# Attention probabilities transposed in 64x128 tiles, and the sinks' products in the two halves of the array

## The chip, the cores and the metric

The kernel runs on one core of one Trainium2 chip. The time is the device time of the program in microseconds (us); the median of three runs is compared. The engines are named as in the profile: PE is TensorE (matmuls; PEld its weight loads), DVE is VectorE, ACT is ScalarE, POOL is GpSimd, SP is SyncE, which issues most of the transfers.

## What is computed

Attention over 4 batches, 8 heads, 768 positions and heads of 64, in which a query sees the last 128 positions and the first 4 (the sinks), and behind it a gated convolution of the 512 wide result with two projections. Cut to what matters:

```python
scores = scale * np.matmul(q, k.transpose(0, 1, 3, 2))
keep = is_sink | in_window              # pos < 4, or 0 <= rel < 128
a = np.exp(np.where(keep, scores, -1e9) - max)
a = a / (np.sum(a, axis=-1, keepdims=True) + 1e-09)
attn = np.matmul(a, v)
...
gate = 1.0 / (1.0 + np.exp(-causal_conv5(x, conv_w)))
return gate * (x @ w_val) @ w_out       # x: attn, heads side by side
```

## The kernel before

The work is cut into 24 steps: 4 batches, 3 blocks of 256 query positions (`p`), 2 groups of four heads (`qd`). In a step the four heads are two pairs `g` of two heads `j`; the 256 positions are two chunks `c` of 128. Two steps (both `qd`) make one unit `m` of the gated part, of which there are 12.

One step goes through these stages; the short names are those of the order table, the lines those of the profile:

- `s0`, `s1` (L391): scores of a pair of heads on TensorE, in tiles of 64 rows by 32 columns, eight of which fit in the array, into one of two PSUM pairs of banks (`pr`). VectorE merges the window's two triangles (L396) and takes the maxima (L400, or L405 in the first `qd`).
- `e0`, `e1` (L416): exponentials on ScalarE with their sums; `rec` (L422, L423): the reciprocal.
- `norm` (L431 to L438): GpSimd multiplies by it. The window's probabilities go to a tile `wx` as two halves `n` of 64 key columns each; those of the sinks go to `skb`, in three parts (the value, its rounded part, the difference).
- `tx` (L449): TensorE transposes `wx`. For each `n`, `g` and `c` one transpose of 128 query positions by 128 (two heads of 64 key columns), with the 128x128 identity: eight in a step. The data are the weights that are loaded, the identity is what streams. The results fill both banks of a `pr` pair, half `n` in bank `n`.
- `px` (L477, L479): VectorE copies bank 0 twice into the tile `wt`, masked for the current and for the earlier block; `py` (L486): ScalarE copies bank 1. So the two engines read one bank each.
- `sk` (L454), `ts` (L462 or L464): the sinks' probabilities are transposed (128x128) and copied out into `skt`, masked by chunk.
- `vl` (L504): the product with the values in tiles of 64x64, four in the array: rows by head `j`, columns by the place in the output; PSUM bank by pair `g`. Each of them runs over one, two or three blocks of 64 queries.
- `si` (L511): the sinks' product is added: for each pair `g` one matmul of 128x128 weights (`vh`, L257 and L259, from the transfer `vsk`) over 256 positions. `vh` holds the sinks' values of both pairs, with zeros for the pair that is not meant.
- `xc`, `xh`, `hd`, `xl` (L518, L526, L530, L534): the result is copied out and split into a high and a low part; `c4`, `c0`, `c1` (L539, L547) and `th` are the convolution and the gate.
- `v0` to `v3` (L566): the value projection of a unit, 12 matmuls of 128x128 weights over 256 positions each; `g`, `h`, `l` (L585, L591, L595) gate it and split it; `o0` to `o3` (L606): the output projection, six matmuls over 512 columns each; `t0`, `t1` (L610, L613): the result is copied and stored.

Around these stand the decoding of the two weight matrices (`wva.0` to `wof.3`, L137 to L183) in the first part, some matmuls of zeros (`fill`, L224), and the loads `kq`, `vv`.

All engines follow one table, `ORDER`: a list of some thousand event names, written out, in which each event emits its instructions in the order of the list, with no scheduler behind it. So each engine's queue is fixed by that list, and semaphores set the rest. Scores and transposes share the two `pr` pairs in turn; `sk`, the projections and the weights' decoding share two other banks.

A mark such as `128*128` behind a matmul in the profile is the shape of the tile of the array that it uses, rows by columns. Below, a "change of shape" is a matmul whose tile has another shape than that of the matmul ahead.

Of the kernel before, what the change touches and what calls it, by code (L numbers as in the profile page):

```python
# [37 lines left out]
wvc.0 s1.0 wve.0 fill.4 wva.1 wvb.1 e0.0 wva.2 e1.0 wvb.2 wvc.2 fill.7 wvd.1 wol.0 kq.2 s1.1 wvc.1 rec.0 wvl.3
s0.1 fill.10 s1.2 wvf.0 woa.0 e1.1 wve.1 e0.1 wob.0 norm.0 tx.0 px.0 e1.2 woc.0 rec.1 py.0 vv.0 fill.6 sv.0
sk.0 ts.0 wod.0 wva.3 norm.1 s0.2 e0.2 vl.0 kq.8 kq.3 s0.3 wvf.1 si.0 xc.0 woe.0 wvb.3 xh.0 tx.1 c4.0 rec.2  # L40
wof.0 wol.2 wol.1 wvc.3 fill.6 hd.0 wvd.2 wve.2 px.1 wvd.3 kq.4 wve.3 e0.3 c0.0 c1.0 woa.1 wob.1 wvf.2 norm.2
vv.3 py.1 vv.1 sv.1 xl.0 tx.2 py.2 sk.1 px.2 woc.1 ts.1 vl.1 s1.3 wvf.3 wod.1 si.1 xc.1 c4.1 sk.2 ts.2 s0.4
hd.1 xh.1 xl.1 c0.1 woe.1 e1.3 wol.3 rec.3 woa.3 c1.1 wob.3 e0.4 v0.0 v1.0 th.0 y0.0 norm.3 vv.2 g0.0 vl.2
woa.2 wob.2 h0.0 l0.0 th.1 s1.4 kq.6 kq.5 wof.1 woe.3 e1.4 v2.0 v3.0 y1.0 tx.3 py.3 si.2 xc.2 woe.2 hd.2 xh.2
g1.0 px.3 wof.2 wod.2 s0.6 c4.2 c0.2 h1.0 o0.0 l1.0 o2.0 e0.6 wof.3 s0.5 c1.2 rec.4 xl.2 s1.6 wod.3 o1.0 o3.0
t0.0 norm.4 sk.3 e0.5 ts.3 t1.0 vl.3 si.3 xh.3 xc.3 xl.3 s1.5 e1.6 tx.4 px.4 vv.5 sk.4 ts.4 hd.3 c4.3 c0.3
e1.5 rec.5 norm.5 v0.1 v1.1 y0.1 py.4 c1.3 th.2 v2.1 v3.1 g0.1 h0.1 kq.7 s0.7 vv.4 th.3 vl.4 y1.1 g1.1 vv.6
l0.1 s1.7 rec.6 sv.6 s1.8 h1.1 si.4 xh.4 l1.1 xc.4 hd.4 e0.7 o2.1 o3.1 c4.4 c0.4 xl.4 e1.8 kq.10 kq.9 c1.4
norm.6 tx.5 o0.1 t1.1 py.5 o1.1 px.5 sk.5 e1.7 tx.6 rec.7 px.6 ts.5 t0.1 py.6 vl.5 si.5 xc.5 hd.5 xh.5 s0.9
e0.9 sk.6 ts.6 s0.8 e0.8 c4.5 c0.5 c1.5 xl.5 vv.7 v0.2 rec.8 v1.2 norm.7 tx.7 py.7 px.7 th.4 g0.2 v2.2 s1.9  # L50
s1.10 norm.8 th.5 h0.2 e1.9 vl.6 si.6 sk.7 vv.8 v3.2 ts.7 xc.6 hd.6 xh.6 l0.2 g1.2 rec.9 o0.2 c4.6 h1.2 l1.2
# [795 lines left out]
```

## Time and profile before

| | |
|---|---|
| median of 3 runs | 271.12 us (270.26 to 271.2) |
| the profiled execution: its time | 270.55 us |
| its span, first to last instruction | 268.7 us |
| TensorE busy | 258.3 us, 96%, 3760 matmuls |
| VectorE, ScalarE, GpSimd busy | 205.4, 189.1, 176.2 us |
| granted TensorE clock, mean | 0.991 |
| last matmul ends at | about 262 us |

The profile is one execution on the chip. Its groups name a line, an engine, an operation, `out<-in` and the shape, then how often it ran, the busy time and the mean length of one, then the idle time of the engine just ahead of it and who ended that. The length of a matmul in it contains the way through the array, so the lengths of neighbours overlap; a pace is read from start to start. A transposing matmul (L449, L454) is one record; one of full 32-bit numbers that isn't transposing (L391, L504) is two.

### The profile page before, as it was taken

The numbers are of one execution on the slowest core, as the hardware profiler recorded it, in microseconds if no ns is written. First come the engines' busy times: TensorE is split into PE (matmuls) and PEld (weight loads), VectorE is DVE, ScalarE is ACT, GpSimd is POOL, SyncE is SP. The second block draws the span as 40 slices with busy tenths as digits, with TensorE's granted clock in tenths as the row PEclk, the third lists the DMA queues.
The fourth block names the chain that finished last, engine by engine and source line by source line (L and its number), as shares of the span: only waits on it lengthen the run. The fifth ranks groups of instructions, "written<-read, shape, count | busy, mean of one in ns | idle before, by whom it ended". The sixth has DMA issues, their size and how long they took to land.

```text
span 268.7 us, 9474 instructions
## 1 busy us (share of the span) xinstructions
PE 258.3 (96%) x3760; PEld 213.6 (79%) x3760; DVE 205.4 (76%) x561; ACT 189.1 (70%) x667; POOL 176.2 (66%) x233
## 2 busy tenths in 40 slices
PE   7899999999999999999999999999999999999990
PEld 3356578789879888879879889889879889898970
DVE  6977989979869878998778788889478857834530
ACT  3899998897888867857676778968567757442420
POOL 6187986876948785675669464895776774816330
PEclk9999999999999999999999999999999999999996
DMA  7998633039344043318833619053335211040202
GB/s 220 370 384 267 239 105 104 0 112 348 107 133 168 1 158 120 131 40 290 262 115 98 196 66 305 3 146 115 111 132 201 59 44 40 1 139 2 78 14 75
DMA packets 27394, 36.93 MB, mean 137 GB/s; under 512 B 2256, under 2 KB 23760, under 8 KB 27344
## 3 DMA queue, kind: packets, MB, share of 16 engines
q1 hardware_dynamic: 26528, 35.48, 39.9%
q10 hardware_dynamic: 816, 0.79, 0.9%
q8 instruction: 31, 0.51, 0.8%
q14 instruction: 19, 0.16, 0.2%
HBM read 29.97 MB, written 6.29 MB: 135 GB/s over the span
## 4 chain that ended last, share of the span: by engine, by line
PE 83%; ACT 9%; POOL 2%; DMA 2%; issue 1%; DVE 0%; POOLq 0%; ACTq 0%
PE ac L606 25%; PE ac L566 25%; PE xv L504 11%; PE pr L391 10%; PE pr L449 7%; ACT w L416 4%; PE xv L511 3%; DMA raw<-in_w_val_dram 2%; PE ac L454 1%; POOL xl L534 1%; ACT wvh L151 1%; ACT wv_p L137 1%; ACT wv_p L156 1%; ACT wvl L183 1%; POOL wo_f L157 0%
## 5 line engine op out<-in xcount | busy, mean ns | idle before, releaser
L547 DVE SCALAR_TENSOR_TENSOR sg<-xv,cw,sg 128x256 f32<-128x256 f32 x192 | 77.8, 474 | 12.4 <-POOL sg L539 7.0
L431 POOL TENSOR_TENSOR wx<-w,sm 128x512 f32<-128x512 f32 x48 | 49.1, 1044 | 11.3 <-DVE sm L423 11.1
L416 ACT ACTIVATE w<-pr,ngm 128x132 f32<-128x132 f32 x136 | 48.5, 369 | 1.7
L595 POOL TENSOR_TENSOR gl<-sg,gh 128x512 fp32r<-128x512 f32 x24 | 31.0, 1295 | 28.1 <-ACT gh L591 28.0
L566 PE MATMUL ac<-xh,wvh 128*128 128x256 f32 x192 | 48.4, 286 | 0.0
L566 PE MATMUL ac<-xh,wvl 128*128 128x256 f32 x192 | 47.1, 279 | 0.0
L606 PE MATMUL ac<-woh,gh 128*128 128x512 f32 x96 | 39.2, 408 | 0.0
L539 POOL TENSOR_TENSOR sg<-xt,cw 128x512 f32<-128x512 f32 x24 | 25.0, 1043 | 20.6 <-ACT xt L518 20.6
L606 PE MATMUL ac<-wol,gh 128*128 128x512 f32 x96 | 38.0, 396 | 0.0
L606 PE MATMUL ac<-woh,gl 128*128 128x512 f32 x96 | 38.0, 395 | 0.0
L566 PEld LDWEIGHTS ac<-xh,wvh 128*128 128x128 f32 x192 | 36.1, 188 | 0.8 <-issue 0.5
L566 PEld LDWEIGHTS ac<-xh,wvl 128*128 128x128 f32 x192 | 36.2, 188 | 0.2
L391 PE MATMUL pr<-k,q 64*32 64x168 f32 x1536 | 35.3, 307 | 0.7 <-DMA q<-in_qt_dram 0.6
L504 PEld LDWEIGHTS xv<-wt,v 64*64 64x64 f32 x1024 | 30.4, 133 | 7.0 <-issue 4.5
L504 PE MATMUL xv<-wt,v 64*64 64x192 f32 (+2 forms) x1024 | 34.5, 278 | 0.2 <-PE ac L566 0.2
L534 POOL TENSOR_TENSOR xl<-xt,xh 128x512 fp32r<-128x512 f32 x24 | 30.8, 1289 | 3.2 <-ACT xh L526 2.8
L566 PE MATMUL ac<-xl,wvh 128*128 128x256 f32 x192 | 30.7, 280 | 0.4 <-POOL xl L534 0.4
L391 PEld LDWEIGHTS pr<-k,q 64*32 64x32 f32 x1536 | 23.8, 106 | 7.9 <-issue 2.6
L396 DVE COPY_PREDICATED pr<-low,pr 128x256 f32<-128x256 uint8 x48 | 20.3, 423 | 12.2 <-PE pr L391 12.2
L591 ACT ACTIVATE gh<-sg 128x512 fp32r<-128x512 f32 x24 | 15.0, 628 | 19.2 <-DVE sg L585 19.2
L416 ACT ACTIVATION_READ_ACCUMULATOR w<-pr,ngm 128x1 f32 x136 | 27.6, 203 | 0.0
L518 ACT ACTIVATE xt<-xv 128x512 f32<-128x512 f32 x24 | 14.4, 600 | 17.3 <-PE xv L511 17.2
(135 smaller groups left out, 495.6 us busy)
## 6 DMA issues: line engine op xcount, KB each, us to landing
k<-in_kt_dram SPq DMA_DIRECT2D x23, 408.0 KB, 5.2
v<-in_vt_dram SPq DMA_DIRECT2D x16, 384.0 KB, 4.5
out_dram<-osb SPq DMA_DIRECT2D x24, 256.0 KB, 2.2
q<-in_qt_dram SPq DMA_DIRECT2D x23, 256.0 KB, 5.4
raw<-in_w_out_dram SPq DMA_DIRECT2D x4, 512.0 KB, 6.7
v<-in_vt_dram SPq DMA_DIRECT2D x8, 256.0 KB, 5.2
raw<-in_w_val_dram SPq DMA_DIRECT2D x3, 512.0 KB, 7.3
vs<-in_vsk_dram SPq DMA_DIRECT2D x8, 128.0 KB, 5.1
```

The costliest lines, as they stand in the source:

```text
L391: nc.tensor.matmul(ss[e * QB:(e + 1) * QB, j, c * n + x0:c * n + x1], q[js, g, (4 * c + e) * QB:(4 * c + e + 1) * QB], k[js, g, (2 * c + e ...
L396: nc.vector.copy_predicated(sv[:, :, :, :D], low[:, None, None, :].to_broadcast([P, 2, 2, D]), sv[:, :, :, 2 * HB:])
L416: nc.scalar.activation(out=w[:, g, j, c], in_=sx[:, j, c, :PK], func=AF.Exp, scale=0.125 if whole else -1.0, bias=ngm[:, g, j, c:c + 1], a ...
L431: nc.gpsimd.tensor_tensor(out=t[:, n].rearrange("p c h x -> p h c x"), in0=w[:, :, :, at], in1=sm.to_broadcast([P, 4, 2, D]), op=ALU.mult)
L449: nc.tensor.transpose(out=x[:, n, o:o + P], identity=ident, in_=ws[s][:, n, c, 2 * g:2 * g + 2].rearrange("p j x -> p (j x)"))
L504: nc.tensor.matmul(acc[o * D:(o + 1) * D, g, x0 + h * D:x0 + (h + a1 - a0 + 1) * D], v[js, g, n], t[js, g, n, a0:a1 + 1].rearrange("p a r ...
L534: nc.gpsimd.tensor_tensor(out=half(xls, s, "xl", F32R), in0=xts[s], in1=half(xhs, s, "xh", F32R).bitcast(F32), op=ALU.subtract)
L539: nc.gpsimd.tensor_tensor(out=half(sg, s, "sg", F32), in0=xts[s], op=ALU.mult, in1=cw[:, g, KT - 1:].to_broadcast([P, 2, PQ]))
L547: nc.vector.scalar_tensor_tensor(out=g, in0=x, scalar=a, in1=g, op0=ALU.mult, op1=ALU.add)
L566: nc.tensor.matmul(acc[:, h], a[:, kc, cs], x[:, kc], start=(n == 0), stop=(n == 11))
L595: nc.gpsimd.tensor_tensor(out=gl, in0=g, in1=gh.bitcast(F32), op=ALU.subtract)
L606: nc.tensor.matmul(acc, a[:, kc, ts], x[:, kc], start=(kc + n == 0), stop=(kc + n == 5))
```

## The change

Three things change.

The transposes: `tx` makes 16 transposes a step instead of eight, each of 64 query positions (one half `r` of the partitions) by 128, with a 64x64 block of the identity. Rows 0 to 63 use the upper half of the array, 64 to 127 the lower, with all 128 columns: a tile of 64x128. The half `r` goes to PSUM bank `r`. So `px` and `py` read both banks, and the layout of `wt` follows: `px` stays two operations of the same sizes, `py` becomes two copies, one for each half.

The sinks: `skb` is ordered by pair `g` first, so that after the transpose pair 0 lies in partitions 0 to 63 and pair 1 in 64 to 127. The product `si` of a pair then needs 64 rows, and the two pairs' matmuls use the two halves of the array, each into its own bank. `vsk` and `vh` become half as large (no zeros for the other pair), and the correction of `vh`'s third part becomes two operations on GpSimd.

The order: the table `ORDER` is written anew. The lines behind it move by one, from the transposes on by 3 to 7: L391 is now L392, L449 is L452, L454 is L460, L504 is L510, L511 is L518, L566 is L573, L606 is L613, L486 is L491.

```diff
-NR = 8 * NSK
+NR = 4 * NSK
...
-blanks wvl.0 load_conv kq.0 masks signs leads fill.5 wvl.1 conv_weights wvl.2 wva.0 wvb.0 s0.0 kq.1 wvd.0
+fill.5 blanks load_conv masks signs leads wvl.0 kq.0 conv_weights wva.0 wvb.0 wvc.0 wvl.1 wvd.0 s0.0 s1.0
...
-            vraw[b, qd] = x = p2.tile([P, 2, P], F32, name="vs", tag="vs", bufs=2)
+            vraw[b, qd] = x = p2.tile([P, P], F32, name="vs", tag="vs", bufs=2)
...
-        vs[b, qd] = h = p2.tile([P, 2, P], F32R, name="vh", tag="vh", bufs=3)
+        vs[b, qd] = h = p2.tile([P, P], F32R, name="vh", tag="vh", bufs=3)
         nc.scalar.activation(out=h, in_=x, func=AF.Copy)
-        r = slice(2 * NR, 3 * NR)
-        nc.gpsimd.tensor_tensor(out=h[r], in0=x[r], in1=h[r].bitcast(F32), op=ALU.subtract)
+        for g in range(2):
+            r = slice(g * D + 2 * NR, g * D + 3 * NR)
+            nc.gpsimd.tensor_tensor(out=h[r], in0=x[r], in1=h[r].bitcast(F32), op=ALU.subtract)
...
-        sk = [skb[s % 2][:, n * NR:(n + 1) * NR] for n in range(3)]
-        nc.gpsimd.tensor_tensor(out=sk[0].rearrange("p (h c n) -> p h c n", c=2, n=NSK), in0=w[:, :, :, D:HB],
-                                in1=sm.to_broadcast([P, 4, 2, NSK]), op=ALU.mult)
+        sk = [skb[s % 2].rearrange("p (g k r) -> p k g r", g=2, r=NR)[:, n] for n in range(3)]
+        w, sm = (x.rearrange("p g j c x -> p g (j c) x") for x in (wn[s][0], wn[s][2][:, :, :, :, None]))
+        nc.gpsimd.tensor_tensor(out=sk[0].rearrange("p g (h n) -> p g h n", n=NSK), in0=w[:, :, :, D:HB],
+                                in1=sm.to_broadcast([P, 2, 4, NSK]), op=ALU.mult)
...
-                    o = (2 * g + c) * P
-                    nc.tensor.transpose(out=x[:, n, o:o + P], identity=ident,
-                                        in_=ws[s][:, n, c, 2 * g:2 * g + 2].rearrange("p j x -> p (j x)"))
+                    for r in range(2):
+                        rs, o = slice(r * D, (r + 1) * D), (4 * n + 2 * c + g) * D
+                        nc.tensor.transpose(out=x[:, r, o:o + D], identity=ident[rs, rs],
+                                            in_=ws[s][rs, n, c, 2 * g:2 * g + 2].rearrange("p j x -> p (j x)"))
+
+    def turned(s, n):
+        return trs[s].rearrange("p r (n x d) -> p n r x d", n=2, x=4)[:, n]
...
     def probs_x(s):
-        h0 = 2 if steps[s][1] == 0 else 0
-        t = prob(s)
-        x = trs[s][:, 0].rearrange("p (g h r) -> p g h r", g=2, r=D)
-        nc.vector.tensor_tensor(out=t[:, :, 2:6, 0], in0=x, in1=cur[:, None, None, :].to_broadcast([P, 2, 4, D]),
-                                op=ALU.mult)
-        nc.vector.tensor_tensor(out=t[:, :, h0:4, 2], in0=x[:, :, h0:],
-                                in1=prev[:, None, None, :].to_broadcast([P, 2, 4 - h0, D]), op=ALU.mult)
+        c0 = 1 if steps[s][1] == 0 else 0
+        t, x = prob(s), turned(s, 0)
+        for k, c, a, m in ((1, 0, 0, cur), (c0, c0, 2, prev)):
+            nc.vector.tensor_tensor(out=t[:, :, k:k + 2 - c, :, a].rearrange("p r k g d -> p r (k g) d"),
+                                    in0=x[:, :, 2 * c:], op=ALU.mult,
+                                    in1=m[:, None, None, :].to_broadcast([P, 2, 4 - 2 * c, D]))
...
     def probs_y(s):
-        h0 = 1 if steps[s][1] == 0 else 0
-        t = prob(s)
-        x = trs[s][:, 1].rearrange("p (g h r) -> p g h r", g=2, r=D)
-        nc.scalar.activation(out=t[:, :, 1 + h0:5, 1], in_=x[:, :, h0:], func=AF.Copy)
+        t, x = prob(s), turned(s, 1)
+        for r in range(2):
+            c = 1 if steps[s][1] + r == 0 else 0
+            nc.scalar.activation(out=t[:, 1 - r, r + c:r + 2, :, 1].rearrange("p k g d -> p (k g) d"),
+                                 in_=x[:, r, 2 * c:], func=AF.Copy)
...
         for g in range(2):
-            nc.tensor.matmul(accs[s][:, g, KT - 1:], vs[b, qd][:, g],
-                             skt[s].rearrange("p c r -> p (c r)"), start=False, stop=True, skip_group_check=True)
+            gs = slice(g * D, (g + 1) * D)
+            nc.tensor.matmul(accs[s][:, g, KT - 1:], vs[b, qd][gs], skt[s][gs].rearrange("p c r -> p (c r)"),
+                             start=False, stop=True, skip_group_check=True)
```

What the new table does to the engines' queues is seen in the built programs' orders (each row an instruction, `xN` for N alike; no time is in it). TensorE before, around the transposes of step 3: the end of a value projection, the transposes, the sinks' products of step 2, the scores of a later step, an output projection.

```order
L566 MATMUL ac_93<-xl,wvh 128x256 x4
L449 MATMUL pr_87<-ident,wx 128x128 x8
L511 MATMUL xv<-skt,vh 128x256 x2
L391 MATMUL pr_86<-k,q 32x168 x16
L606 MATMUL ac_92<-woh,gh 128x512
L606 MATMUL ac_92<-wol,gh 128x512
```

The same place afterwards:

```order
L573 MATMUL ac_93<-xl,wvh 128x256 x4
L518 MATMUL xv<-skt,vh 128x256 x2
L452 MATMUL pr_87<-ident,wx 128x64 x16
L392 MATMUL pr_86<-k,q 32x168 x16
L613 MATMUL ac_92<-woh,gh 128x512
L613 MATMUL ac_92<-wol,gh 128x512
```

The sinks and the transposes have changed places and now have one shape, so the shape changes ahead of the pair and behind it; before, it changed only around the scores. TensorE near the end of the program before (values and sinks of step 21, transposes of step 23):

```order
L504 MATMUL xv<-wt,v 64x128 x4
L504 MATMUL xv<-wt,v 64x64 x4
L511 MATMUL xv<-skt,vh 128x256 x2
L449 MATMUL pr_87<-ident,wx 128x128 x8
L606 MATMUL ac_93<-woh,gh 128x512
L606 MATMUL ac_93<-wol,gh 128x512
```

And afterwards:

```order
L510 MATMUL xv<-wt,v 64x64 x4
L452 MATMUL pr_86<-ident,wx 128x64 x16
L452 MATMUL pr_87<-ident,wx 128x64 x16
L518 MATMUL xv<-skt,vh 128x256 x2
L613 MATMUL ac_93<-woh,gh 128x512
L613 MATMUL ac_93<-wol,gh 128x512
```

The transposes of two steps now stand together with the sinks' products, with one change of shape ahead of all three and one behind. ScalarE around the copy `py` of an early step before (`vc`, `sg`, `gh` belong to the gated part):

```order
L422 ACTIVATE sm<-sm 128x8
L572 ACTIVATE vc<-ac_93 128x512
L486 ACTIVATE wt<-pr_86 128x2x4x64
L552 ACTIVATE sg<-sg 128x512
L591 ACTIVATE gh<-sg 128x512
```

And afterwards:

```order
L579 ACTIVATE vc<-ac_92 128x512
L598 ACTIVATE gh<-sg 128x512
L491 ACTIVATE wt<-pr_86 128x4x64 x2
L417 ACTIVATE w,sm<-sx,ngm 128x132 x4
L559 ACTIVATE sg<-sg 128x512
```

One copy of 512 elements a partition has become two of 256, and four exponentials now stand directly behind it.

More of the change, by code (lines that the diff above doesn't have):

```diff
@@ L36 @@
 ORDER = """
-blanks wvl.0 load_conv kq.0 masks signs leads fill.5 wvl.1 conv_weights wvl.2 wva.0 wvb.0 s0.0 kq.1 wvd.0
[L38 to L51, printed above, removed]
@@ L77 @@
-ts.23 v2.10 v3.10 g0.10 c4.22 hd.22 c0.22 c1.22 th.21 g1.10 h0.10 l0.10 o2.10 vv.23 vl.23 h1.10 si.23 xc.23
-hd.23 xh.23 l1.10 xl.22 o0.10 o1.10 c4.23 c0.23 xl.23 t0.10 c1.23 o3.10 v0.11 th.22 v1.11 t1.10 v2.11 v3.11
-g0.11 th.23 g1.11 h0.11 l0.11 o2.11 h1.11 l1.11 o0.11 o1.11 flag t0.11 o3.11 t1.11
+fill.5 blanks load_conv masks signs leads wvl.0 kq.0 conv_weights wva.0 wvb.0 wvc.0 wvl.1 wvd.0 s0.0 s1.0
+fill.10 wve.0 wva.1 wvl.2 wvb.1 e0.0 wva.2 wvd.1 e1.0 wvc.1 wvb.2 wvf.0 wvc.2 kq.1 s0.1 rec.0 norm.0 fill.7
@@ new lines @@
+e0.1 wol.0 woa.0 kq.2 s1.1 e1.1 s1.2 e1.2 fill.4 wve.1 tx.0 fill.6 wob.0 woc.0 px.0 vv.0 sv.0 sk.0 kq.4 s0.2
+py.0 rec.1 norm.1 ts.0 kq.3 vl.0 wvl.3 wva.3 s0.3 si.0 wod.0 woe.0 e0.2 xh.0 wvf.1 tx.1 xc.0 wof.0 c4.0 hd.0
+fill.6 wvb.3 rec.2 wvc.3 px.1 wvd.2 wve.2 kq.6 wvd.3 e0.3 wve.3 vv.1 wol.1 norm.2 wvf.2 woa.1 c0.0 py.1 tx.2
+c1.0 vv.3 sv.1 py.2 sk.1 wob.1 ts.1 woc.1 px.2 vv.2 wod.1 vl.1 s1.3 wvf.3 si.1 xc.1 c4.1 sk.2 ts.2 s0.4 hd.1
+xh.1 c0.1 xl.0 e1.3 rec.3 c1.1 wol.3 woa.3 kq.7 wob.3 th.0 woe.1 wof.1 xl.1 v0.0 v1.0 y0.0 norm.3 g0.0 wol.2
@@ new lines @@
+vl.8 si.8 e0.12 vv.12 vv.10 xc.8 hd.8 c4.8 xh.8 s1.11 e0.11 e1.11 kq.15 xl.8 sk.9 ts.9 c0.8 c1.8 th.7 v2.3
+v3.3 g1.3 h1.3 o2.3 s1.12 s1.13 e1.12 norm.10 l1.3 rec.12 vl.9 si.9 xc.9 c4.9 tx.10 hd.9 px.10 o3.3 xh.9
+rec.11 xl.9 norm.11 py.10 c0.9 c1.9 o0.3 t1.3 o1.3 t0.3 sk.10 ts.10 s0.13 tx.11 py.11 e0.13 px.11 vl.10 si.10
+v0.4 v1.4 xc.10 hd.10 xh.10 c4.10 sv.12 th.9 kq.18 c0.10 vv.11 norm.12 th.8 g0.4 vv.13 c1.10 kq.14 v2.4 h0.4
+v3.4 g1.4 sk.11 l0.4 ts.11 tx.12 vl.11 py.12 px.12 s0.14 h1.4 s1.14 si.11 scalars sk.12 ts.12 th.10 e1.13
@@ new lines @@
+rec.13 l1.4 o0.4 o1.4 xc.11 hd.11 c4.11 sv.13 xh.11 vv.14 e0.14 o2.4 e1.14 c0.11 o3.4 t1.4 c1.11 s0.18 s0.15
+vl.12 t0.4 th.11 si.12 xc.12 hd.12 norm.13 tx.13 xl.10 px.13 xh.12 xl.11 v2.5 rec.14 c4.12 v3.5 v0.5 py.13
+v1.5 c0.12 e0.18 c1.12 g1.5 g0.5 e0.15 norm.14 warm_up sk.13 ts.13 xl.12 h0.5 s1.15 e1.15 s1.18 l0.5 vl.13
+si.13 o0.5 kq.16 rec.15 kq.19 s0.16 tx.14 vv.17 px.14 h1.5 xc.13 hd.13 xh.13 th.12 l1.5 e0.16 c4.13 o2.5 o3.5
+o1.5 py.14 vv.15 c0.13 c1.13 t1.5 sk.14 ts.14 xl.13 e1.18 s1.16 rec.18 kq.20 vl.14 t0.5 si.14 xc.14 hd.14
@@ new lines @@
+norm.15 xh.14 tx.15 px.15 e1.16 py.15 c4.14 sk.15 ts.15 kq.17 c0.14 c1.14 rec.16 norm.16 v0.6 vv.16 v1.6 v2.6
+g0.6 s0.17 s0.19 th.13 h0.6 e0.17 xl.14 vl.15 si.15 l0.6 v3.6 g1.6 s1.19 xc.15 hd.15 kq.21 h1.6 l1.6 s1.17
+xh.15 sk.16 ts.16 o0.6 tx.16 xl.15 c4.15 e1.19 o1.6 px.16 c0.15 c1.15 kq.22 e1.17 norm.18 rec.17 vv.19 th.14
+v0.7 v1.7 s0.20 norm.17 g0.7 t0.6 py.16 vl.16 e0.19 rec.19 si.16 xc.16 hd.16 xh.16 tx.18 sk.18 ts.18 px.18
+c4.16 c0.16 c1.16 e0.20 py.18 xl.16 th.15 h0.7 v2.7 v3.7 g1.7 l0.7 tx.17 o2.6 o3.6 py.17 px.17 s1.20 s0.21
@@ new lines @@
+xc.20 hd.20 xh.20 xl.18 e0.23 v0.9 v1.9 e1.23 g0.9 h0.9 c4.20 c0.20 c1.20 o3.8 v2.9 norm.22 v3.9 rec.23 t1.8
+g1.9 h1.9 sk.21 l0.9 norm.23 ts.21 vl.21 tx.22 py.22 tx.23 px.23 si.21 xc.21 hd.21 px.22 l1.9 xh.21 vv.23
+c4.21 py.23 o2.9 o3.9 o0.9 c0.21 c1.21 t1.9 o1.9 t0.9 xl.21 th.21 sk.22 xl.20 ts.22 vl.22 si.22 xh.22 sk.23
+ts.23 xc.22 v0.10 c4.22 th.20 hd.22 v1.10 g0.10 c0.22 c1.22 v2.10 v3.10 h0.10 l0.10 xl.22 o2.10 g1.10 h1.10
+vl.23 l1.10 si.23 o0.10 xc.23 hd.23 c4.23 xh.23 c0.23 o1.10 t0.10 xl.23 o3.10 c1.23 v0.11 t1.10 th.22 v1.11
@@ L80 @@
+g0.11 h0.11 th.23 l0.11 v2.11 v3.11 g1.11 flag o2.11 h1.11 l1.11 o0.11 o1.11 t0.11 o3.11 t1.11
 """
```

50 lines of the change are left out of this document (20 added, 30 removed).

## Prediction, made before the changed kernel was run

> **What bounds the kernel now.** I read the page first, then the busy time in three stretches, then TensorE's groups by form, then single stretches of its timeline.
>
> ```profile
> span 268.7 us, 9474 instructions
> PE 258.3 (96%) x3760; PEld 213.6 (79%) x3760; DVE 205.4 (76%) x561; ACT 189.1 (70%) x667; POOL 176.2 (66%) x233
> PEclk9999999999999999999999999999999999999996
> PE 83%; ACT 9%; POOL 2%; DMA 2%; issue 1%; DVE 0%; POOLq 0%; ACTq 0%
> PE ac L606 25%; PE ac L566 25%; PE xv L504 11%; PE pr L391 10%; PE pr L449 7%; ACT w L416 4%; PE xv L511 3%; DMA raw<-in_w_val_dram 2%; PE ac L454 1%; POOL xl L534 1%; ACT wvh L151 1%; ACT wv_p L137 1%; ACT wv_p L156 1%; ACT wvl L183 1%; POOL wo_f L157 0%
> ```
>
> TensorE is busy 96% of the span at full granted clock, and the chain that ended last is its work. A high busy share alone would not prove it, since matmuls overlap; the stretches do (columns: stretch, its length, busy time of PE, PEld, DVE, ACT, POOL with counts, clock, DMA share, GB/s):
>
> ```profile
> 0.00:41.00 41.00, 37.62 (x483) 21.77 (x484) 33.75 (x101) 35.43 (x128) 29.75 (x54) 1.00 0.76 259
> 41.00:262.00 221.00, 220.67 (x3281) 191.80 (x3281) 171.70 (x461) 153.32 (x541) 146.40 (x180) 1.00 0.36 117
> ```
>
> From 41 us to the end of the products TensorE lacks 0.33 us in 221; all real waiting is in the first 41 us. So nothing but TensorE's own work sets the time there: what is taken off its stream comes off the time, as long as the others keep delivering. The question is what the stream costs, instruction by instruction.
>
> **The transposes.** Groups by form give the two kinds that change, with their weight loads:
>
> ```profile
> L449 PE MATMUL pr<-ident,wx 128*128 128x128 f32 x192 | 25.2, 274 | 0.3 <-ACT w L416 0.3
> L511 PE MATMUL xv<-skt,vh 128*128 128x256 f32 x48 | 11.8, 328 | 0.0
> L449 PEld LDWEIGHTS pr<-ident,wx 128*128 128x128 f32 x192 | 21.7, 141 | 2.8 <-POOL wx L431 0.9 <-issue 0.8
> L504 PEld LDWEIGHTS xv<-wt,v 64*64 64x64 f32 x1024 | 30.4, 133 | 7.0 <-issue 4.5 <-PE ac L606 0.6 <-ACT wt L486 0.6
> ```
>
> A mean duration contains the pipeline, so I take paces from runs of instructions. This is one step's block between two kinds of block, in the timeline (start, length, count):
>
> ```profile
> 113.42 0.29 PE L504 MATMUL xv<-wt,v 64*64 64x64 f32 x8
> 113.64 0.50 PE L511 MATMUL xv<-skt,vh 128*128 128x256 f32 x2
> 113.98 1.04 PE L449 MATMUL pr<-ident,wx 128*128 128x128 f32 x8
> 114.78 0.48 PE L606 MATMUL ac<-woh,gh 128*128 128x512 f32 x1
> ```
>
> Eight transposes last 1.04 us, one lasts 0.274: seven intervals of 0.109 us. The pace of one is 0.109, and 24 steps x 8 x 0.109 = 20.9 us are on the path now. What limits that pace, the 128 streamed columns or the load of 128 weight columns, decides the change, which halves the first (64 columns of the identity) and not the second. The loads by themselves, first of transposes, then of the value projection:
>
> ```profile
> 58.22 0.20 PEld L449 LDWEIGHTS pr<-ident,wx 128*128 128x128 f32 x2 [0.26 <-issue]
> 79.97 0.19 PEld L566 LDWEIGHTS ac<-xh,wvh 128*128 128x128 f32 x1 [0.27 <-issue]
> 80.08 0.19 PEld L566 LDWEIGHTS ac<-xh,wvl 128*128 128x128 f32 x1
> ```
>
> One transposing load lasts 0.141, two 0.20: the second follows after 0.06 us, against 0.11 in the projection. So the transposing load takes about 0.06, and the 0.109 is the streaming; half the columns should take 0.055. On this the Trainium skill differs (TensorE: Matmul & The Clock Gate, section LDWEIGHTS): a load's time is its column count over 1.2 GHz whatever the rows, 0.107 us for 128. The projection's rows agree with it, the transposing rows do not; by the rule alone the new pairs would keep the old pace and the sum would be 10.0 us higher.
>
> Whether two halves of the array run side by side is seen in the one block that uses four quarters, two in each half (L504; the lines are of growing windows, so each pair differs by four instructions, one in each quarter):
>
> ```profile
> 104.80 0.45 PE L504 MATMUL xv<-wt,v 64*64 64x128 f32 x12
> 104.80 0.51 PE L504 MATMUL xv<-wt,v 64*64 64x128 f32 x16
> 103.76 0.15 PEld L504 LDWEIGHTS xv<-wt,v 64*64 64x64 f32 x4 [0.27 <-issue]
> 103.76 0.21 PEld L504 LDWEIGHTS xv<-wt,v 64*64 64x64 f32 x8 [0.27 <-issue]
> ```
>
> Four more matmuls of 64 columns add 0.06 us, four more loads add 0.06: matmuls and loads of all four quarters overlap. Four loads end in 0.15 where one lasts 0.133, so each starts some 0.007 after the one ahead. A round of two half-height transposes I therefore put at 0.057 (bounds: 0.055, half of 0.109, and 0.109, no gain): 24 x 8 x 0.057 = 10.9 us. **Saved: 10.0 us.**
>
> **The sinks' products.** Their pace when nothing is exposed is that of the same shape in L566, here 48 in one piece of the chain, 0.117 us each:
>
> ```profile
> 59.43 5.61 PE ac L566 x48
> ```
>
> Two in a row become two side by side, so 24 x 0.117 = **2.8 us saved** (bounds 0 and 2.8; no row shows this weight type in halves, and I take the upper one by L504). The late start of the second half costs 48 blocks x 0.007 = 0.3 us.
>
> **What the new shape costs: changes of tile shape.** Their price stands in rows (start, length, count):
>
> ```profile
> 56.74 0.40 PE L504 MATMUL xv<-wt,v 64*64 64x128 f32 x11
> 57.06 0.50 PE L511 MATMUL xv<-skt,vh 128*128 128x256 f32 x2
> 57.49 0.80 PE L391 MATMUL pr<-k,q 64*32 64x168 f32 x32
> 58.23 1.09 PE L449 MATMUL pr<-ident,wx 128*128 128x128 f32 x8
> 59.16 0.27 PE L454 MATMUL ac<-ident,skb 128*128 128x128 f32 x1
> 79.24 0.80 PE L391 MATMUL pr<-k,q 64*32 64x168 f32 x32
> 79.97 0.39 PE L566 MATMUL ac<-xh,wvh 128*128 128x256 f32 x1
> 80.20 0.28 PE L566 MATMUL ac<-xh,wvl 128*128 128x256 f32 x1
> 80.31 0.28 PE L566 MATMUL ac<-xh,wvh 128*128 128x256 f32 x1
> ```
>
> The sinks' block, both times behind L504, takes 0.43 us to the start of L391 (another shape) but 0.34 to L449 (the same shape) in the earlier fence: 0.09 us to let the array run empty. Then the first load of the new shape is not hidden: in L566 the second matmul comes 0.23 after the first instead of 0.11, so 0.11 us; for transposes 58.23 to 59.16 is 0.93 against 8 x 0.109 = 0.87, so 0.06. Before, transposes and sinks have the shape of their neighbours (128x128); afterwards they differ from everything but each other. Counted over all of TensorE's rows in the two built orders, changes of shape go from 95 to 138: 43 x 0.09 = 3.9 us. Among the blocks entered by a change, products with 128 loaded columns go from 29 to 45 (16 x 0.11 = 1.8 us) and transposes from 6 to 29 (23 x 0.06 = 1.4 us); scores (34) and values (24) stay, and the few bf16 ones are left out. **Added: 7.1 us.**
>
> No row shows a change in which only the height of the tile differs (128x128 to 64x128): I take the price of the others, and nothing as the other bound. The Trainium skill (TensorEngine Tiling (Array Packing), Key Properties) says that a change of tiling mode, not of tile, drains the TensorE; L511's 0.09 us agrees where width and height change together, and it makes the full price the likelier one here.
>
> **Edits off the path.** These rows are ScalarE's and GpSimd's:
>
> ```profile
> L486 ACT ACTIVATE wt<-pr 128x512 f32<-128x512 f32 x16 | 9.6, 598 | 4.8 <-PE pr L449 2.9 <-DVE wt L479 1.4 <-PE ac L606 0.5
> L486 ACT ACTIVATE wt<-pr 128x384 f32<-128x384 f32 x8 | 4.0, 494 | 0.9 <-PE pr L449 0.5 <-DVE wt L479 0.2
> L257 ACT ACTIVATE vh<-vs 128x256 fp32r<-128x256 f32 x8 | 3.3, 418 | 0.5 <-DMA vs<-in_vsk_dram 0.5
> L462 ACT ACTIVATE skt<-ac,blk 128x128 fp32r<-128x128 f32 x12 | 3.8, 382 | 0.0
> PEld xv L504 <- ACT wt L486: 0.6, 2, 0.3
> ```
>
> The copy `py` becomes two: 256 + 256 elements instead of 512 (2 x 418 - 598 = 238 ns, 16 steps), 128 + 256 instead of 384 (382 + 418 - 494 = 306 ns, 8 steps): 3.8 + 2.4 = 6.3 us more on ScalarE, which is busy 70%. Behind the copies on ScalarE stand the exponentials and the copies of other steps; the value products L504 wait for `py`, and did so twice, 0.6 us in all. In the new order the product still stands far behind: I cost it at nothing, at most 6.3 us if that cover is gone. `px` keeps its count and sizes on VectorE; the sinks' three GpSimd operations keep 32 elements a row; the sinks' values are half as large to load and copy, with one more small subtraction in 8 steps, on an engine busy 66%. The order of the first 41 us moves too; its waiting of 3.4 us could change by a microsecond either way.
>
> **Sum.** -10.0 - 2.8 + 0.3 + 7.1 = -5.4 us. The profiled execution took 270.55 us (span 268.7, so 1.85 around it); it becomes 265.1. The median of the three runs is 271.12, 0.57 higher, and the same subtraction gives **265.7 us**.
>
> **The rivals.**
> 1. *The transposes keep the pace of 0.109 a round* (slower): the load in half height loses its quick form, or the two halves' loads come one after the other. The place is L449's new line, the price 24 x 8 x 0.052 = 10.0 us, the time 275.7. It decides from a round of 0.085 us on (0.057 + 5.4 / 192). For it: no row has a transposing load in a half; against it: 0.06 in the load rows and the overlap in L504. Chance 0.13. (The rule of the Trainium skill on loads, quoted above from TensorE: Matmul & The Clock Gate, would give this time.)
> 2. *New waits take the gain*: `py`'s 6.3 us lie on the path, since TensorE now comes 0.2 us sooner per step, or the new order puts a producer too close. All of it gives 272.0, half of it 268.8. For it: other engines have less time per step than before; against it: 0.6 us of waiting for `py` now, and a gapless 221 us. Chance 0.14.
> 3. *A change of height alone is free*: 41 of the 138 changes lie between 128x128 and 64x128; without their draining and bare loads 6.9 us more go, 258.8. Only the absence of such a row speaks for it. Chance 0.07.
>
> **How the numbers follow.** The forecast has 0.66, and by itself 263.5 to 268 (a round of 0.055 to 0.07). Half a per cent, 1.4 us, is what a measurement can tell here. The range of 262.5 to 271.0 holds the forecast and nearly all of rival 2, 0.80; rivals 1 and 3 lie outside it with 0.20. Faster by more than that: 0.66 + 0.07 + 0.06 of rival 2 = 0.79. The same: 0.07 of rival 2. Slower: 0.13 + 0.01 = 0.14.
>
> **What would show it.** Right: 16 transposes of a step in about 0.65 us from first start to last end (0.46 of rounds and a tail of 0.2), the two sinks' products starting within 0.01 us of each other, a projection's second matmul 0.23 after its first behind a transpose block, TensorE still without gaps after 41 us. Transposes spaced 0.055 one by one mean rival 1; idle time of L510's loads put down to the ScalarE copy means rival 2; transposes starting 0.1 us behind a projection's last matmul without an empty array mean rival 3. The forecast is wrong above 269.8 or below 262.

## The result, and the profile after

| | before | after |
|---|---|---|
| median of 4 runs each | 270.84 us (270.26 to 271.2) | 267.55 us (267.09 to 268.28) |
| ratio, 95% interval | | 0.9883 [0.9853, 0.9914] |
| the profiled execution: its time | 270.55 us | 267.7 us |
| its span | 268.7 us | 265.9 us |
| last matmul ends at | 261.7 us | 258.9 us |

The change saves 3.3 us. The forecast was 265.7 us, a saving of 5.4. From one profiled execution to the other 2.85 us are saved; the working below goes by these two. Executions over 1.5% longer than a kernel's fastest, at a lower granted clock, are left out of the ratios, and in x1, where they are four of ten, out of its median too.

The page of after begins with the same picture as before (span, busy time, granted clock, the chain by engine):

```profile
span 265.9 us, 9900 instructions
PE 253.8 (95%) x3948; PEld 204.7 (77%) x3952; DVE 205.6 (77%) x561; ACT 188.9 (71%) x691; POOL 177.6 (67%) x241
PEclk9999999999999999999999999999999999999998
PE 80%; ACT 11%; POOL 3%; DMA 2%; issue 1%; DVE 0%; ACTq 0%; POOLq 0%
```

TensorE is 4.5 us less busy, but the span is only 2.8 us shorter, and ScalarE and GpSimd hold more of the chain (11 and 3% for 9 and 2%). The stretches show on which side the difference lies, and the last piece of the chain when the products end (start, length, what):

```profile
0.00:41.00 41.00, 36.31 (x495) 20.44 (x500) 34.19 (x101) 34.88 (x124) 30.11 (x56) 1.00 0.77 256
41.00:260.00 219.00, 217.47 (x3455) 184.31 (x3454) 171.37 (x461) 153.99 (x567) 147.52 (x186) 1.00 0.37 117
...
253.27 5.61 PE ac L613 x24
```

The values of step 2 (L510) start at 41.61 us, where before had 40.96. Up to that start TensorE is busy 36.92 us, before 37.58: it had less to do, and nothing came of that. In the second stretch TensorE lacks 1.53 us up to 260, of which 1.14 come after its last matmul, which ends at 258.86; 0.39 are waits, and these are new.

The blocks themselves. One step's transposes behind the sinks, in the timeline (the place answers to 113.42 of before):

```profile
112.78 0.51 PE L510 MATMUL xv<-wt,v 64*64 64x128 f32 x16
113.22 0.39 PE L518 MATMUL xv<-skt,vh 64*128 64x256 f32 x2
113.44 0.65 PE L452 MATMUL pr<-ident,wx 64*128 64x64 f32 x16
114.02 0.50 PE L613 MATMUL ac<-woh,gh 128*128 128x512 f32 x1
```

Sixteen transposes last 0.65 us, one lasts 0.227: seven rounds to the start of the last pair, 0.061 each. The two sinks' products end together, 0.39 us for both where one lasts 0.381. And L452 starts 0.22 behind L518, which was 0.34 before: 0.12 saved. Where the transposes of a step stand alone between two blocks of the output projection, the price of the new shape is seen. The place before:

```profile
71.36 0.40 PE L606 MATMUL ac<-woh,gl 128*128 128x512 f32 x1
71.60 1.04 PE L449 MATMUL pr<-ident,wx 128*128 128x128 f32 x8
72.39 0.48 PE L606 MATMUL ac<-woh,gh 128*128 128x512 f32 x1
72.71 0.39 PE L606 MATMUL ac<-wol,gh 128*128 128x512 f32 x1
```

And after:

```profile
71.38 0.39 PE L613 MATMUL ac<-wol,gh 128*128 128x512 f32 x1
71.61 0.40 PE L613 MATMUL ac<-woh,gl 128*128 128x512 f32 x1
71.94 0.71 PE L452 MATMUL pr<-ident,wx 64*128 64x64 f32 x16
72.58 0.50 PE L613 MATMUL ac<-woh,gh 128*128 128x512 f32 x1
72.92 0.40 PE L613 MATMUL ac<-wol,gh 128*128 128x512 f32 x1
```

In a steady run the projection starts a matmul every 0.23 us. From the one ahead of the transposes to the second behind them there are 1.35 us before and 1.31 after; less the two of the projection, the eight transposes cost 0.88 and the sixteen 0.84. Eight rounds of 0.061 are 0.49 of that; 0.35 us go to the two changes of shape (0.10 to let the array run empty ahead, seen as 0.33 instead of 0.23, and the rest behind). A block that stands alone has gained 0.04 us. The saving comes from the blocks that share their changes of shape with the sinks or with other transposes: at 113 us, from the first sinks' product to the projection, 1.14 us before (113.64 to 114.78) have become 0.80.

TensorE's groups by form, and its waits (what waited, for whom, us in all, times, longest):

```profile
L452 PE MATMUL pr<-ident,wx 64*128 64x64 f32 x384 | 17.2, 227 | 1.4 <-POOL wx L432 1.2 <-ACT w L417 0.3
L518 PE MATMUL xv<-skt,vh 64*128 64x256 f32 x48 | 9.3, 381 | 0.1
...
PE pr L452 <- POOL wx L432: 1.2, 3, 0.5
PE ac L573 <- POOL xl L541: 0.7, 1, 0.7
PE xv L510 <- ACT wt L491: 0.4, 1, 0.4
```

The copy `wt` (L491), which the second rival named, is waited for once, 0.4 us. These three, GpSimd's among them, all lie ahead of step 2's values. Behind them the trace has three short pauses: 0.15 us at 57.57 for `skt` (ScalarE), 0.13 at 81.26 for `xl` (GpSimd) and 0.11 at 164.31 for a transfer of `q`.

### The profile page after: what moved, and what is told of

Read it like the earlier page. It is cut to its first block, busy times and chain, and to the rows that moved or that the text cites. A ratio compares the mean times of both kernels' runs of the same rounds, so it can differ in the third digit from the quotient of the medians.

```text
span 265.9 us, 9900 instructions
## 1 busy us (share of the span) xinstructions
PE 253.8 (95%) x3948; PEld 204.7 (77%) x3952; DVE 205.6 (77%) x561; ACT 188.9 (71%) x691; POOL 177.6 (67%) x241
## 4 chain that ended last, share of the span: by engine, by line
PE 80%; ACT 11%; POOL 3%; DMA 2%; issue 1%; DVE 0%; ACTq 0%; POOLq 0%
PE ac L613 26%; PE ac L573 25%; PE xv L510 11%; PE pr L392 9%; PE pr L452 5%; ACT w L417 4%; PE xv L518 3%; DMA raw<-in_w_val_dram 2%; POOL xl L541 1%; PE ac L460 1%; ACT wv_p L156 1%; POOL sg L546 1%; ACT wv_p L137 1%; ACT wvh L151 1%; ACT wt L491 1%
## 5 line engine op out<-in xcount | busy, mean ns | idle before, releaser
L573 PE MATMUL ac<-xh,wvh 128*128 128x256 f32 x192 | 48.5, 287 | 0.0
L573 PE MATMUL ac<-xh,wvl 128*128 128x256 f32 x192 | 47.1, 279 | 0.0
L613 PE MATMUL ac<-woh,gh 128*128 128x512 f32 x96 | 39.7, 413 | 0.0
L613 PE MATMUL ac<-woh,gl 128*128 128x512 f32 x96 | 38.0, 396 | 0.0
L613 PE MATMUL ac<-wol,gh 128*128 128x512 f32 x96 | 38.0, 396 | 0.0
L573 PEld LDWEIGHTS ac<-xh,wvh 128*128 128x128 f32 x192 | 36.4, 190 | 1.3 <-issue 0.5
L573 PEld LDWEIGHTS ac<-xh,wvl 128*128 128x128 f32 x192 | 36.1, 188 | 0.2
L392 PE MATMUL pr<-k,q 64*32 64x168 f32 x1536 | 35.5, 307 | 0.7 <-DMA q<-in_qt_dram 0.6
L510 PEld LDWEIGHTS xv<-wt,v 64*64 64x64 f32 x1024 | 30.3, 133 | 6.9 <-issue 4.1
L510 PE MATMUL xv<-wt,v 64*64 64x192 f32 (+2 forms) x1024 | 34.5, 278 | 0.4 <-ACT wt L491 0.4
L573 PE MATMUL ac<-xl,wvh 128*128 128x256 f32 x192 | 31.0, 281 | 0.9 <-POOL xl L541 0.7
L392 PEld LDWEIGHTS pr<-k,q 64*32 64x32 f32 x1536 | 23.8, 106 | 7.7 <-issue 1.9
L573 PEld LDWEIGHTS ac<-xl,wvh 128*128 128x128 f32 x192 | 26.0, 188 | 1.5 <-POOL xl L541 1.4
```

The lines of the kernel that those rows point to most:

```text
L392: nc.tensor.matmul(ss[e * QB:(e + 1) * QB, j, c * n + x0:c * n + x1], q[js, g, (4 * c + e) * QB:(4 * c + e + 1) * QB], k[js, g, (2 * c + e ...
L510: nc.tensor.matmul(acc[o * D:(o + 1) * D, g, x0 + h * D:x0 + (h + a1 - a0 + 1) * D], v[js, g, n], t[js, n % 2, n // 2, g, a0:a1 + 1].rearr ...
L573: nc.tensor.matmul(acc[:, h], a[:, kc, cs], x[:, kc], start=(n == 0), stop=(n == 11))
L613: nc.tensor.matmul(acc, a[:, kc, ts], x[:, kc], start=(kc + n == 0), stop=(kc + n == 5))
```

## The experiments

The theory at the outset was the forecast's with its sizes mended: TensorE's own stream sets the time, a round costs 0.062 us and each change of shape its full price. The rivals: the new table brings or takes waits of its own; ScalarE's second copy costs what the forecast set at nothing; GpSimd is the nearer bound. Each kernel is compared with the kernel before, run beside it on the same chip; the ratio is to that. Where TensorE's "stream" is given below, it is the time from the start of step 2's values to the end of the last matmul in the profiled execution, and the gaps are what TensorE idles in it.

**The table and the shapes, each alone.** Two kernels exchange the table:

```diff
 # x1_old_order: the code of after
-ORDER = (the table of after)
+ORDER = (the table of before)
 # x2_new_order: the code of before
-ORDER = (the table of before)
+ORDER = (the table of after)
```

The old table under the new shapes. 

> The changed kernel with the order table of before. TensorE's stream by the rows (a round of transposes 0.062, each change of shape 0.093 and the bare load behind it) is 3.4 us shorter than before and 1.4 longer than with the new table: 145 changes of shape against 138. Theory (the missing gain was eaten where the first 41 us wait for a chain of engines, whatever the order): that part gains nothing here either, 268.5 to 269.5 us. Rival (the new table brought the waiting): the whole 3.4 us show, 267.4 us or less.

Measured: 269.48 us, the median of six runs from 268.87 to 272.28 (of all ten: 271.14); ratio 0.9961 [0.9927, 0.9995]. That is the upper end of what the theory expected; the rival's 267.4 was not reached. So the new shapes gain something with the old table too, and 1.9 us less than with the new one, but the size isn't settled by these runs, and of the six no trace was kept.

The new table under the old shapes. 

> The kernel of before with the new order table. Stream 0.2 us longer than before, 97 changes of shape against 95. Theory: 270.5 to 271.5 us, the table alone is worth nothing. Rival (the new table brings waiting of its own): 272 us or more, with idle time of TensorE after 41 us as in the changed kernel.

Measured: 272.03 us, 1.0041 [1.0021, 1.0061]: 1.2 us slower than before. The rival held. TensorE's stream takes 222.09 us for 220.71, of which 1.04 are gaps where before has none, and it starts 0.27 later. With the old shapes the new table costs; why is not shown.

**The transposes and the sinks, each alone, with the new table.**

```diff
 # x3_transposes_only: the code of after, the sinks at full height
-            nc.tensor.matmul(accs[s][:, g, KT - 1:], vs[b, qd][gs], skt[s][gs].rearrange("p c r -> p (c r)"),
+            nc.tensor.matmul(accs[s][:, g, KT - 1:], vs[b, qd][:, g], skt[s].rearrange("p c r -> p (c r)"),
...
 # x4_sinks_only: the code of after, the transposes and copies of before
+                    o = (2 * g + c) * P
+                    nc.tensor.transpose(out=x[:, n, o:o + P], identity=ident,
+                                        in_=ws[s][:, n, c, 2 * g:2 * g + 2].rearrange("p j x -> p (j x)"))
...
```

> The changed kernel with the sinks' products at full height again (zeros in the other pair's rows, 128 x 128 weights). Stream 1.7 us longer than the changed kernel's: 2.9 us of product come back, 5 changes of shape go. Theory: 269.0 to 269.6 us. Rival (the sinks' halves bring nothing, since their changes of shape cost what they save): 267.6 us as the changed kernel.

Measured: 271.56 us, 1.0018 [0.9999, 1.0037], 2 us above what was expected. TensorE's stream without its gaps took 1.9 us more than after's (218.79 for 216.86), near what the prices of the forecast said (1.7). The rest of the 3.3 us between the two profiled executions is waiting: the stream starts 0.56 later and has 1.40 us of gaps for 0.39. Over the whole span these waits stand out:

```profile
PE pr L452 <- POOL wx L432: 1.8, 4, 0.5
PE ac L572 <- POOL xl L540: 1.0, 2, 0.7
PE xv L517 <- POOL vh L260: 0.9, 2, 0.6
```

All of them are for GpSimd (after has 1.2, 0.7 and, for `vh`, none on the list). This kernel keeps the zeros in `vh`, and it corrects them with the two subtractions of after on 256 columns: GpSimd work that neither before nor after has. So it isn't the transposes alone, and the last pair of experiments takes that up.

> The changed kernel with the transposes of before (eight of 128 x 128, one copy by ScalarE), only the sinks' products in halves. Stream 1.3 us longer than before: 2.8 us saved, but 120 changes of shape instead of 95 cost 4.0. Theory: 271.5 to 273 us, slower than before. Rival (the two parts add up, each with its own gain): 268 us.

Measured: 273.11 us, 1.0081 [1.0052, 1.0109], slower than before, as expected, 0.1 above the range: 2.8 us of work are taken away, but the sinks now stand in a shape of their own, with a change ahead of them and behind. TensorE's stream without its gaps is 222.05 us, 1.3 more than before, the size that the prices gave. The two halves of the change need each other: the changes of shape that either brings alone they share.

**The overlap of the two halves.**

```diff
 # x6_halves_in_turn: after, the loop over the halves outermost
-        for n in range(2):
-            for g in range(2):
-                for c in range(2):
-                    for r in range(2):
+        for r in range(2):
+            for n in range(2):
+                for g in range(2):
+                    for c in range(2):
```

> The changed kernel, but each step's 16 transposes go first all through the upper half of the array, then all through the lower, so no two neighbours can run side by side. Theory (the gain is the overlap of the halves, a transpose alone takes a load's 0.058 us): a block lasts 0.43 us more, 16 x 0.058 instead of 8 x 0.062, 24 x 0.43 = 10.4, of which the first three steps are hidden: 276 to 278 us. Rival (the gain is that 64 columns stream in half the time, and the halves don't matter): no change, 267.6.

Measured: 273.78 us, 1.0102 [1.0063, 1.0142], 6.2 us above after and below the 276 to 278 that were expected. A block in its timeline, behind the sinks:

```profile
46.64 0.39 PE L518 MATMUL xv<-skt,vh 64*128 64x256 f32 x2
46.87 0.96 PE L452 MATMUL pr<-ident,wx 64*128 64x64 f32 x16
47.76 0.80 PE L392 MATMUL pr<-k,q 64*32 64x168 f32 x32
```

0.96 us from first start to last end for 0.65: the same sixteen transposes, 24 x 0.3 = 7 us, of which 6.2 are in the time. The overlap is what the saving consists of, and it hangs on consecutive instructions lying in different halves. Not all of it goes, though: sixteen at a distance of 0.061 would have taken 15 x 0.061 + 0.22 = 1.14. In the trace of this block the starts lie some 0.06 us apart, but near the change of half three pairs start within 0.01 us of each other (at 0.241 and 0.248 from the first, 0.359 and 0.368, 0.423 and 0.429): there both halves ran side by side.

**ScalarE's second copy.** x5 lays `wt` out so that one copy does for both halves; x8 splits the copy of before; x7 is x5 with a table in which some transposes stand elsewhere.

```diff
 # x5_one_copy: after
...
-        for r in range(2):
-            c = 1 if steps[s][1] + r == 0 else 0
-            nc.scalar.activation(out=t[:, 1 - r, r + c:r + 2, :, 1].rearrange("p k g d -> p (k g) d"),
-                                 in_=x[:, r, 2 * c:], func=AF.Copy)
+        u = t[:, 0, 0, 1, 1]
+        nc.scalar.activation(out=bass.AP(u.tensor, u.offset, [u.ap[0], [9 * D, 2], [6 * D, 4], [1, D]]),
+                             in_=x, func=AF.Copy)
...
 # x8_split_copy: before
-        nc.scalar.activation(out=t[:, :, 1 + h0:5, 1], in_=x[:, :, h0:], func=AF.Copy)
+        for g in range(2):
+            nc.scalar.activation(out=t[:, g, 1 + h0:5, 1], in_=x[:, g, h0:], func=AF.Copy)
```

> The changed kernel with the tile of the transposed probabilities laid out so that ScalarE's copy is one instruction of 512 elements again (in the first block it also copies 128 elements that nobody reads). Theory (the first 40 us are ScalarE's: its chain is gapless there, and two copies instead of one lie on it in three steps; after that they lie beside TensorE): the value products of step 2 start 0.5 to 0.8 us sooner, the rest is as long as in the changed kernel, 266.6 to 267.2 us against 267.6. Rival (the second copy is on the path in all 24 steps): 264 us or less. Second rival (it is never on the path): 267.6, no change.

Measured: 267.49 us, 0.988 [0.9849, 0.991], the time of after: the second rival held.

> The kernel of before, with ScalarE's copy of the transposed probabilities cut into two instructions (one for each pair of heads), nothing else: the suspected cost alone, 0.24 to 0.31 us more on ScalarE in each step. Theory: only the three steps ahead of 40 us pay, 0.5 to 0.9 us: 271.4 to 271.8 us. Rival (each step pays): 5 us or more. Second rival (never on the path): no change.

Measured: 271.0 us, 0.9996 [0.9975, 1.0017], the time of before; the second rival held here too. The second copy is covered, in both kernels; the forecast's "nothing" for it holds, and the second rival's first half is gone.

> As the kernel with one copy, and the transposes of steps 5, 10, 16 and 18 one or two places earlier on TensorE, where a change of shape is there anyway: 133 changes instead of 136 by the table, 0.65 us of draining and bare loads less. Theory (changes of shape cost 0.15 to 0.2 us each wherever TensorE sets the time): 0.4 to 0.7 us below the kernel with one copy. Rival (such waits are hidden): the same time.

Measured: 270.31 us, 0.9985 [0.9964, 1.0007], 2.8 us above x5. In this kernel the transposes of step 16 are moved past scores that then get their banks, so from there on part of the computation is another one. The profile shows gaps of 2.97 us behind step 2's values where x5 has 0.20, in front of transposes above all. It says nothing on the price of a change of shape, for which it was made.

**The first 41 us.** The matmuls of zeros (`fill`) are left out, all of them in x9 and half in x11: TensorE work that nothing uses, all within the first 28 us.

```diff
 # x9_no_fill
-        for _ in range(n):
+        for _ in range(0):
 # x11_half_fill
-        for _ in range(n):
+        for _ in range(n // 2):
```

> The changed kernel without the 38 matmuls of zeros that the order puts into the first 27 us (they only keep TensorE busy and no output needs them): 8.1 us less of work on TensorE there, at 0.215 each. Theory (up to about 40 us ScalarE and GpSimd set the time, not TensorE): not over 1 us shorter, 266.6 to 268.5 us if the granted clock stays; the clock may fall in the longer gaps, and then it is longer by some us, seen in the clock's row. Rival (TensorE sets this stretch as it sets the rest): 259 to 261 us.

Measured: 268.91 us, 0.9918 [0.9892, 0.9944]. Eight microseconds of TensorE's work are gone, and the kernel is 1.4 us slower than after. Its first stretch:

```profile
0.00:41.00 41.00, 30.81 (x463) 17.63 (x464) 34.35 (x101) 34.88 (x124) 30.64 (x56) 0.96 0.76 256
```

TensorE is busy 30.81 us there, not 36.31, and step 2's values still start at 41.36, not 41.61. The clock granted in this stretch is 0.96, not 1.00: it was halved from 14.6 to 18.0 us.

> The same with about half of these matmuls of zeros left (18 of 38; 4.3 us less of work), so that the clock has less reason to fall. Theory: within 0.7 us of the changed kernel, 266.9 to 268.3 us. Rival: 263 to 264 us.

Measured: 267.92 us, 0.9881 [0.9843, 0.9919], the time of after, with 4.3 us less for TensorE to do; step 2's values start at 41.16. So what TensorE saves before 41 us is worth nothing in the time.

**GpSimd.** x10 is x5 with the sinks of twelve steps at full height, at the places where that was thought to save changes of shape; x12 has all of them in halves again, but keeps x10's full-size `vh`, half of which nothing uses then.

```diff
 # x10_mixed_sinks and x12_full_vh, against x5_one_copy
+FULL = (0, 1, 5, 6, 10, 11, 13, 15, 19, 20, 22, 23)      # x10
+FULL = ()                                                # x12
...
-        vs[b, qd] = h = p2.tile([P, P], F32R, name="vh", tag="vh", bufs=3)
+        vs[b, qd] = h = p2.tile([P, 2, P], F32R, name="vh", tag="vh", bufs=3)
...
-            gs = slice(g * D, (g + 1) * D)
-            nc.tensor.matmul(accs[s][:, g, KT - 1:], vs[b, qd][gs], skt[s][gs].rearrange("p c r -> p (c r)"),
+            gs = slice(0, P) if s in FULL else slice(g * D, (g + 1) * D)
+            nc.tensor.matmul(accs[s][:, g, KT - 1:], vs[b, qd][gs, g], skt[s][gs].rearrange("p c r -> p (c r)"),
```

> The kernel with one copy, in which 12 steps have the sinks' products in halves (where the transposes or scores stand next to them, so that the shape changes there anyway) and 12 have them at full height with zeros (where a 128x128 matmul follows). By the rows, 7 of these save a change worth 0.093 + 0.106 for 0.117 more of product (0.08 us each) and 5 one worth 0.093 + 0.056 (0.03 us each). Theory (a change of height alone costs the full price): 0.7 us below the kernel with one copy, 266.5 to 267.1 us. Rival (a change of height alone is nearly free): 12 x 0.117 = 1.4 us longer, 268.9 us.

Measured: 270.42 us, 0.9991 [0.9971, 1.0012]. Both missed.

> The one-copy kernel (267.5 us) with all sinks' products in halves, as there, but with the sinks' values laid out at full size again: vsk, vh and the copy and subtraction that make vh are twice as large (ScalarE 0.42 instead of about 0.3 us, GpSimd's two subtractions on 256 columns instead of 128, eight times a run), and half of vh is never used. TensorE's stream is that of the one-copy kernel. Theory (the larger work on vh, which on GpSimd stands ahead of the normalisation, delays the transposes; this is where the two kernels with sinks at full height lost their 2 us beyond the stream): 269 to 270, with TensorE waiting at L453 for GpSimd's wx some 2 us in all. Rival (the full-height products and their changes of shape are what cost there, the larger vh nothing): 267.2 to 267.9, and the wait for wx as in the one-copy kernel, under 1.3 us. Between the two, 268.0 to 268.9, both count for a part.

Measured: 270.31 us, 0.9978 [0.9964, 0.9993], 2.8 us above x5 with the same TensorE instructions. The theory held, a little above its range. x10 has the same time, so the height of those twelve products made no difference that the times can tell. TensorE's stream without its gaps is 0.6 us shorter in x10 than in x12 (216.86 for 217.44), near the 0.7 of x10's theory and against its rival, which had it longer; that is one execution of each. The subtraction that corrects `vh`, first in before, then in after, then in x12 (x5 has after's):

```profile
L259 POOL TENSOR_TENSOR vh<-vs,vh 32x256 fp32r<-32x256 f32 x8 | 6.2, 779 | 2.6 <-ACT ngm L413 1.8 <-POOL gl L595 0.2 <-POOL sg L539 0.2
```

```profile
L260 POOL TENSOR_TENSOR vh<-vs,vh 16x128 fp32r<-16x128 f32 x16 | 7.8, 485 | 1.2
```

```profile
L261 POOL TENSOR_TENSOR vh<-vs,vh 16x256 fp32r<-16x256 f32 x16 | 12.0, 749 | 1.2 <-POOL sg L546 0.2
```

4.2 us more than after on an engine that is busy two thirds of the span cost 2.8. GpSimd's queue near 195 us in x5 shows how:

```profile
194.16 2.03 POOL L260 TENSOR_TENSOR vh<-vs,vh 16x128 fp32r<-16x128 f32 x4
196.27 2.04 POOL L432 TENSOR_TENSOR wx<-w,sm 128x512 f32<-128x512 f32 x2
```

And in x12 the same place, with TensorE's transposes behind it and the sum of that wait:

```profile
196.03 3.12 POOL L261 TENSOR_TENSOR vh<-vs,vh 16x256 fp32r<-16x256 f32 x4
199.23 2.04 POOL L433 TENSOR_TENSOR wx<-w,sm 128x512 f32<-128x512 f32 x2
...
200.32 0.47 PE L453 MATMUL pr<-ident,wx 64*128 64x64 f32 x8 [0.32 <-POOL wx L433]
201.32 0.40 PE L453 MATMUL pr<-ident,wx 64*128 64x64 f32 x5 [0.53 <-POOL wx L433]
...
PE pr L453 <- POOL wx L433: 2.6, 6, 0.5
```

Four corrections stand in a row ahead of the normalisation that makes `wx`; they take 3.12 us instead of 2.03, and the first half of the transposes waits for the first `wx`, the second half for the second (whose row counts only what starts in the window shown). Of the 3.2 us between the two profiled spans, 0.9 lie ahead of step 2's values (42.22 for 41.30), 1.5 in gaps behind (1.66 for 0.20) and 0.6 in TensorE's rows (217.44 for 216.81). The last may be waiting that is not seen as a gap, because the end of the matmul ahead covers it; that isn't shown. x12 has the copy on ScalarE (0.415 for 0.308 us) and the transfer larger too; the rows put the waits on GpSimd, but the three weren't tried apart. With this, x3 is read as well: less x12's 2.8 us it would be 268.8, where 269.0 to 269.6 was expected; that kernel wasn't run.

## Why the prediction was right, and where it was off

The forecast's direction, its mechanism and its range held; the gain was 3.3 us by the medians, 2.85 from profile to profile, where 5.4 were forecast. The narrower band, 263.5 to 268, holds the result too, but its lower end doesn't follow from the working: a round of 0.055 gives 265.3. By its own steps:

- *The transposing load takes about 0.06, and the halves run side by side*: held, against the first rival. x6 shows the second part by taking it away. The size was a little off: a round is 0.061 to 0.062 us and not 0.057, so 192 rounds save about 9.1 and not 10.0 us. (Whether the halved streaming or the load of 128 columns, 0.06 in the rows of before, sets it now, no run tells.) The rule of the Trainium skill that the prediction cited (TensorE: Matmul & The Clock Gate, section LDWEIGHTS: 0.107 us for 128 columns) is not borne out for these transposing loads: two of them, one in each half, are done in 0.061.
- *The sinks, 0.117 a step*: held; 0.34 became 0.22.
- *43 changes of shape at full price*: held, and the third rival fell with it. Height alone changes between L452 and L613, and the lines at 71 us show the price there. TensorE's stream (stretch, its length, busy time of PE and the rest) was before and is now:

```profile
40.96:261.67 220.71, 220.71 (x3281) 191.84 (x3281) 171.74 (x461) 153.12 (x540) 146.44 (x180) 1.00 0.36 117
41.61:258.86 217.25, 216.86 (x3450) 183.83 (x3449) 170.76 (x461) 153.39 (x566) 146.91 (x186) 1.00 0.37 117
```

  Without gaps that is 3.85 us less. Rounds and sinks of the steps there (21 and 22 of 24) give 8.0 + 2.6, so 6.8 went to changes of shape and late starts, of the 7.4 that the forecast has for the whole run. The streams of x3 and x4, which these prices gave to 0.2 us, say the same.
- *What is taken off its stream comes off the time*, applied to all 24 steps: here the sum failed first. The transposes of three steps and the sinks of two stand ahead of 41 us, where the chain is ScalarE's and then GpSimd's. The prediction had read that all real waiting is there, and yet counted 3 x 0.42 + 2 x 0.12 = 1.5 us of savings in it; x9 and x11 take far more off TensorE there and gain nothing.
- *The first 41 us could change by a microsecond either way*: they did, by 0.65 the wrong way. GpSimd's queue after, there:

```profile
30.08 2.06 POOL L432 TENSOR_TENSOR wx<-w,sm 128x512 f32<-128x512 f32 x2
...
33.58 1.12 POOL L260 TENSOR_TENSOR vh<-vs,vh 16x128 fp32r<-16x128 f32 x2
34.95 1.27 POOL L157 TENSOR_TENSOR wo_f<-wo_e,wo_p 128x512 fp32r<-128x512 f32 x1 [0.26 <-POOL vh L260]
...
37.18 2.54 POOL L541 TENSOR_TENSOR xl<-xt,xh 128x512 fp32r<-128x512 f32 x2
```

And before:

```profile
29.64 2.04 POOL L431 TENSOR_TENSOR wx<-w,sm 128x512 f32<-128x512 f32 x2
...
33.08 0.86 POOL L259 TENSOR_TENSOR vh<-vs,vh 32x256 fp32r<-32x256 f32 x1
...
37.49 1.29 POOL L534 TENSOR_TENSOR xl<-xt,xh 128x512 fp32r<-128x512 f32 x1
```

  From `wx` on, GpSimd works nearly without a pause in both. It begins 0.44 later, the correction of `vh` takes 0.26 longer and 0.26 of waiting follow: `xl` ends at 39.72 instead of 38.78, and the value projection waits for it. Not all of this is the change's: in x5, x6 and x11, with the same table and corrections, this `wx` begins at 29.67 to 29.76, and step 2's values start at 41.16 to 41.44. Nor is it the correction's alone: x2, with the new table and the single subtraction, starts them at 41.23.
- *Edits off the path, with "one more small subtraction in 8 steps, on an engine busy 66%"*: right for ScalarE's copies (x5, x8); for GpSimd it was costed at nothing with no price and no bound, and that doesn't hold in general. x12 shows what more work at that place costs: 2.8 us for 4.2. In after the correction is longer within the late start above; behind it only 0.13 of the 0.39 us of gaps names GpSimd, and not the correction.

The sum, from profile to profile: 3.85 us saved behind step 2's values, less 0.65 of late start, less 0.39 of gaps, is 2.81; what follows the last matmul is 0.04 shorter, which makes 2.85. The 2.55 us that are missing from the forecast are the late start and the gaps, 1.04 in all, and about 1.5 in the stream: 1.5 of savings counted where TensorE isn't the bound and some 0.7 by the longer round, less 0.6 by which the changes of shape came below their 7.4 (some of them lie ahead of 41 us).

How much of the late start is the table's doing and how much the second subtraction's isn't settled. A kernel with one subtraction for both pairs wasn't tried.
